# Evacuating the first layer's products by pairs of blocks, loading the first registers later, and gathering rows one part further ahead, in an attention and mixture-of-experts kernel on one core

## The chip, the core and the metric

The program runs on one core of a Trainium2 chip. The core has TensorE (PE in the rows; PEld is its weight load), VectorE (DVE), ScalarE (ACT), GpSimd (POOL) and SyncE (SP), which run side by side and wait for each other on semaphores. The metric is the device time of one execution in microseconds; a figure for a kernel is the median of its runs.

## What is computed

A random-feature attention makes 4608 rows of 512 numbers, and a mixture of eight experts is applied to these rows. Each row goes to the one expert with the largest gate value; the expert has two layers with a ReLU between them.

```python
# attention: q, k, v are 8 x 8 x 576 x 64, omega is 128 x 64
x_s = x * 64 ** -0.25                                # for x in (q, k)
h = x_s @ omega.T - sum(x_s * x_s) / 2
phi = exp(h - max(h)) / sqrt(128)
kv, z = phi(k).T @ v, sum(phi(k))
attn = (phi(q) @ kv) / (phi(q) @ z + 1e-6)
# experts: w_gate 512 x 8, w1 8 x 512 x 1024, w2 8 x 1024 x 512
logits = x @ w_gate
e = argmax(logits)
gate = softmax(logits)[e]
out[row] = gate * (relu(x[row] @ w1[e]) @ w2[e])
```

## The kernel before

The attention takes the first 250 us, and the change does not touch it. The rows of `x` go to memory (`token_rows`) as they are made. The first 256 rows of the largest expert are worked on in another form while the routing is settled (`products0` to `l21`). All other rows are sorted by expert into **parts** of 384 slots (`T3`), of which the last of an expert may be filled less. `step(t)` works on part t. On these inputs 13 parts run, t = 0 to 12.

**The split numbers.** Each operand of a product is kept as two tiles, a high part (a cast on ScalarE) and a low part (a subtraction on VectorE), and the product of two operands is the sum of high by high, high by low and low by high.

**First layer.** The 1024 hidden units are eight **blocks** f of 128. `l1` makes one block: 4 pieces of the 512 inputs by 3 products, so 12 matmuls of 128x128 weights by up to 384 rows, into one bank of PSUM. The banks are held by two tiles of two banks, `p_1[0]` and `p_1[1]`: blocks 0 and 1 share `p_1[0]`, blocks 2 and 3 `p_1[1]`, blocks 4 and 5 `p_1[0]` again, and so on. `hid` empties a block: ScalarE applies the ReLU and writes the high part to `hb` (`high_low`, L1001), then VectorE writes the low part (L1002). Dependences are followed by whole tile: whatever writes into `p_1[0]` waits for the last reader of `p_1[0]`, whichever of its two banks that read.

**Second layer.** `l2` makes 128 rows of output with 24 matmuls (8 blocks by 3 products); a full part has three of these (a = 2, 1, 0). Where a piece holds 64 rows or fewer, `l2` takes a shorter form (`half`); where a part holds 192 or fewer, the first layer does too (`slim`). Parts 8 and 12 are slim here, part 3 has 320 slots in use, the other parts run with 384.

**What stands around the layers.** The order on each engine is the order in which the code is written (the scheduling is manual).
- POOL: `gather` fetches the rows of a part from memory into `xg`, of which there are two, by three indirect transfers; `weigh` copies the gate values; `out2` scatters results by one indirect transfer for each 128 rows.
- SP: `move` writes the gathered rows to memory and reads them back in another layout (`chunk_rows`, then four transfers into `xq`). Weights of the next expert are loaded with `next(t, 1)` for the first layer and `next(t, 2)` for the second; the latter is issued when the last of the old second-layer weights has been split.
- `xrows(t + 1)`: for each of three pieces VectorE transposes (L952), ScalarE casts the high part (L57), VectorE subtracts the low part (L51). It stands in `begin`, which is written behind the second layer, or, for t = 1 and behind a part of at most 192 rows, in `layer1` behind pair g = 0.
- In a part that begins a new expert (`fresh`) the second-layer weights are split, two blocks before each pair (`split(2, ...)`, two casts and two subtractions).
- `load(t)` reads the row count of part t from `flags` into registers of the engines. `rt.plan` computes `flags` on VectorE just before part 0.

Of the kernel before, what the change touches and what calls it, by code (L numbers as in the profile page):

```python
# [18 lines left out]
P = 128  # L19
# [19 lines left out]
NCH = (NT - T2 + E * (T3 - 1)) // T3  # L39
# [377 lines left out]
class Routing:  # L417
# [99 lines left out]
    def step(self, name, product, f):  # L517

        v = {}
        def made(bank):  # L520
            v["o"] = product(bank)
        def step():
            if "o" not in v:
                made(self.bank(name))
            f(v["o"])
        step.product = made
        return step
# [263 lines left out]
class Experts:  # L791
# [193 lines left out]
            for m in (low, both) if c == NC - 1 else (both, low):  # L985
                m()

    def hid(self, f, n):
        p, k, f = self.bank1(f).unsqueeze(1), n - n % P, slice(f, f + 1)
        self.whole(f, k, p[:, :, :k])  # L990
        if k < n:
            self.half(f, p[:, :, k:n])
# [20 lines left out]
        self.half(f, y[:, :, k:k + HT])  # L1013

    def first(self, n):
        for f in range(self.NF):
            self.split(2, (f,))
            self.l1(0, f, n)
            self.hid(f, n)

    def wide(self, t, g, n):
        for f in (2 * g, 2 * g + 1):
            self.l1(t, f, n)
            self.hid(f, n)

    def slim(self, t, g):
        n = T2 - HT
# [20 lines left out]
    def layer1(self, t):  # L1048
        r = self.r1
        for g in range(self.NF // 2):  # L1050
            def fresh():
                self.split(2, (2 * g, 2 * g + 1))
                if g == self.NF // 2 - 1:
                    self.next(t, 2)
            self.when(self.new, fresh)
            wide = lambda n: lambda: self.wide(t, g, n)
            self.either(r > T2, lambda: self.either(r > T3 - HT, wide(T3), wide(T3 - HT)),
                        lambda: self.either(r > T2 - HT, wide(T2), lambda: self.slim(t, g)))
            if g == 0 and t == 1:
                self.xrows(t + 1)  # L1060
            elif g == 0:
                with self.tc.If(self.before < T2 - HT + 1):
                    self.xrows(t + 1)

# [70 lines left out]
                self.xrows(t + 1)  # L1135

    def step(self, t, following):
        if 0 < t < NCH - 2:
            self.gather(t + 2)
        if t == 0:  # L1140
            self.load(t)
            self.first(T3)
            self.l21()
            self.xrows(1)
            self.gather(2)
            self.next(0, 2)
        else:
            self.layer1(t)
        self.layer2(t)
        if t + 1 < NCH:  # L1150
            self.weigh(t + 1)
        self.nc.gpsimd.drain()
        following()
        r, r2 = self.r3, self.r2
        if t + 1 < NCH:
            self.load(t + 1)
        for a in range(A3 - 1, -1, -1):
            self.out2(t, a, r, r2)
# [108 lines left out]
```

## Time and profile before

| what | us |
| --- | --- |
| median of three runs | 810.91 |
| the three runs | 812.15, 809.96, 810.91 |
| the profiled execution, its own time | 808.02 |
| span of the profiled execution, first to last instruction | 806.3 |
| TensorE busy in the span | 684.1 (85%) |
| VectorE, ScalarE, GpSimd busy | 384.9, 367.8, 269.1 |

The rows of the trace give start, length, engine, line, operation, output and inputs; "x24" is the number of instructions merged in a row, and the bracket says how long the engine had been idle before it and which engine and line ended that. A wait on several semaphores is put down to the one that came last. TensorE's matmuls are pipelined, so the weight loads (PEld) show more exactly when work stood still.

### The profile page before, as it was taken

How to read it: one execution, taken by the hardware profiler on the slowest of the kernel's cores; microseconds unless marked ns; L12 is line 12 of the kernel's file. 1: busy time of each engine (PE TensorE's matmuls, PEld its weight loads, DVE VectorE, ACT ScalarE, POOL GpSimd, SP SyncE). 2: the span in 40 equal slices, each digit the busy share in tenths (PEclk: the TensorE clock that was granted, in tenths of full speed). 3: DMA queues.
4: the chain of work that ended last, by engine and by line, in shares of the span. 5: the costliest groups of instructions: out<-in, count | busy, mean ns of one | idle time of the engine just before them, and what ended most of it. 6: DMA issues, size and time to landing. Idle time of an engine off the chain costs nothing. (4 is left out here: it accounts for less than half of the span.)

```text
span 806.3 us, 19629 instructions
## 1 busy us (share of the span) xinstructions
PE 684.1 (85%) x7011; PEld 610.1 (76%) x7011; DVE 384.9 (48%) x777; ACT 367.8 (46%) x1130; POOL 269.1 (33%) x489
## 2 busy tenths in 40 slices
PE   8999999999999589588879695888887848579795
PEld 6999999998898378577767685777776747478684
DVE  4888888888777642331315413223422542212122
ACT  5999999999894332222223312123322422212121
POOL 6555478777776303203030301120120230020202
PEclk9999999999999899899999998999999879999998
DMA  7676357439312636403234261413352454231300
GB/s 202 183 227 222 81 178 237 136 110 338 145 39 76 180 115 209 137 9 119 43 121 135 83 176 36 133 56 85 132 189 65 127 184 134 59 111 32 94 29 22
DMA packets 92868, 100.54 MB, mean 125 GB/s; under 512 B 28702, under 2 KB 73246, under 8 KB 92064
## 3 DMA queue, kind: packets, MB, share of 16 engines
q1 hardware_dynamic: 85216, 79.27, 32.8%
q0 software_dynamic: 6800, 19.03, 7.3%
q8 instruction: 89, 1.46, 0.8%
q14 instruction: 75, 0.61, 0.3%
q10 hardware_dynamic: 688, 0.16, 0.1%
HBM read 72.12 MB, written 29.77 MB: 126 GB/s over the span
## 5 line engine op out<-in xcount | busy, mean ns | idle before, releaser
L975 PE MATMUL p<-xb,w1p 128*128 128x384 f32 (+1 forms) x1056 | 206.6, 351 | 97.2 <-DVE hb L1002 83.5
L975 PEld LDWEIGHTS p<-xb,w1p 128*128 128x128 f32 x1056 | 191.2, 199 | 112.6 <-DVE hb L1002 96.3
L1084 POOL DMA_INDIRECT out_dram<-ys,idx x38 | 38.4, 1009 | 434.1 <-DVEq L1074 263.0
L1002 DVE SCALAR_TENSOR_TENSOR hb<-p,hb 128x384 fp32r<-128x384 f32 (+1 forms) x88 | 48.0, 545 | 235.2 <-ACT hb L1001 186.7
L1001 ACT ACTIVATE hb<-p 128x384 fp32r<-128x384 f32 (+1 forms) x88 | 42.4, 482 | 193.8 <-PE p L975 191.8
L887 PE MATMUL p<-w2p,hb 128*128 128x512 f32 x552 | 127.1, 389 | 0.0
L887 PEld LDWEIGHTS p<-w2p,hb 128*128 128x128 f32 x552 | 103.6, 188 | 21.5
L191 DVE TENSOR_REDUCE mx<-pp 128x8 f32<-128x1024 f32 x64 | 78.0, 1219 | 10.4 <-PE pp L185 9.7
L199 ACT ACTIVATE qp<-pp,mx 128x128 f32<-128x128 f32 x256 | 77.3, 437 | 0.0
L199 ACT ACTIVATE kp<-pp,mx 128x128 f32<-128x128 f32 x256 | 74.2, 386 | 4.9 <-DVE de L283 1.3
L185 PE MATMUL pp<-omt,th 64*128 64x128 f32 x1024 | 71.7, 280 | 0.2 <-ACT qp_-1_320 L199 0.2
L185 PEld LDWEIGHTS pp<-omt,th 64*128 64x128 f32 x1024 | 63.0, 190 | 0.3 <-ACT qp_-1_320 L199 0.3
L887 PE MATMUL p_1tr<-w2p,hb 128*128 128x512 f32 x240 | 56.4, 390 | 0.0
L211 POOL TENSOR_TENSOR k<-kp 128x256 f32<-128x256 f32 x64 | 46.5, 727 | 24.3 <-ACT kp L199 18.9
L887 PEld LDWEIGHTS p_1tr<-w2p,hb 128*128 128x128 f32 x240 | 44.9, 188 | 9.0
L274 PE MATMUL nu<-kva,qt 128*64 128x73 f32 x1008 | 46.0, 233 | 0.0
L176 DVE COPY th<-tr 128x512 f32<-128x512 f32 x63 | 43.3, 688 | 5.6 <-PE tr L168 3.8
L57 ACT CAST xb<-xgm 128x512 fp32r<-128x512 f32 x21 | 13.0, 620 | 66.8 <-DVE xgm L952 66.8
L243 ACT COPY qt<-t 128x512 f32<-128x512 f32 x64 | 42.2, 660 | 2.0 <-PE t L168 1.6
L274 PEld LDWEIGHTS nu<-kva,qt 128*64 128x64 f32 x1008 | 36.7, 136 | 4.2
L225 PE MATMUL kf<-kp,v 128*64 128x128 f32 x512 | 39.5, 276 | 0.0
L952 DVE STREAM_TRANSPOSE xgm<-xq 128x512 f32<-128x512 f32 x21 | 22.7, 1082 | 31.1 <-DMA xq<-chunk_rows 29.6
(387 smaller groups left out, 1071.7 us busy)
## 6 DMA issues: line engine op xcount, KB each, us to landing
w1s<-in_moe_w_dram SPq DMA_DIRECT2D x5, 2048.0 KB, 8.9
w2s<-in_moe_w_dram SPq DMA_DIRECT2D x5, 2048.0 KB, 9.9
xq<-chunk_rows SPq DMA_DIRECT2D x52, 192.0 KB, 4.2
v<-in_v_dram SPq DMA_DIRECT2D x32, 256.0 KB, 5.6
token_rows<-x SPq DMA_DIRECT2D x8, 1024.0 KB, 8.2
k<-in_k_dram SPq DMA_DIRECT2D x31, 256.0 KB, 5.3
q<-in_q_dram SPq DMA_DIRECT2D x31, 256.0 KB, 5.6
chunk_rows<-xgm SPq DMA_DIRECT2D x7, 768.0 KB, 3.6
```

The source lines that it names most:

```text
L176: self.nc.vector.tensor_copy(t.rearrange("p n (a t) -> p a n t", a=2), s[("tr", h)])
L185: nc.tensor.matmul(o[:, a, n, :], t[r, n, :], self.om[r], start=True, stop=True)
L191: self.nc.vector.tensor_reduce(out=mx, in_=s[("pp", h)], axis=AX.X, op=ALU.max, negate=True)
L199: self.nc.scalar.activation(o[:, j, :], p[:, a, 2 * n + i, :], AF.Exp, bias=mx[:, a, 2 * n + i:2 * n + i + 1])
L211: nc.gpsimd.tensor_tensor(out=k2, in0=kp[:, :2, :], in1=kp[:, 2:, :], op=ALU.add)
L225: nc.tensor.matmul(pkv[c * D:(c + 1) * D, :M], vv, kk, start=n < 2, stop=n > 2)
L243: self.nc.scalar.copy(qt.rearrange("p n (a t) -> p a n t", a=2), s[("t2", h)])
L274: nc.tensor.matmul(o[r, j, :], qt[:, j, r], kva[:, h if h >= 0 else 2 * j + a, :], start=True, stop=True)
L887: self.nc.tensor.matmul(p, x, w[:, c, :], start=c == 0 and x is h and w is self.w2h, stop=c == self.NF - 1 and x is l)
L975: self.nc.tensor.matmul(o, w[:, c, k], x[:, c, :], start=i == 0, stop=i == len(ops) - 1)
L1001: self.nc.scalar.activation(h, p, AF.Relu)
L1002: self.nc.vector.scalar_tensor_tensor(out=l, in0=p, scalar=0.0, in1=h.bitcast(F32), op0=ALU.max, op1=ALU.subtract)
```

## The change

Four things are changed.
1. `hid` takes a pair of blocks. `wide` and `first` now make the products of both blocks, then one ReLU over the two banks (768 numbers for each partition in place of twice 384) and one low part. `first` splits the second-layer weights by two blocks too.
2. `load(0)` stands behind the first layer of part 0 and behind `l21`, no more ahead of them.
3. `gather(t + 2)` at the start of step t becomes `gather(t + 3)` behind `weigh(t + 1)`, ahead of the stores of part t. Step 0 now issues gathers 2 and 3.
4. `xrows` inside `layer1` stands behind pair g = 1, not g = 0.

```diff
-    def hid(self, f, n):
-        p, k, f = self.bank1(f).unsqueeze(1), n - n % P, slice(f, f + 1)
+    def hid(self, g, n):
+        p, k, f = self.p_1[g % 2], n - n % P, slice(2 * g, 2 * g + 2)
         self.whole(f, k, p[:, :, :k])
         if k < n:
             self.half(f, p[:, :, k:n])
...
     def first(self, n):
-        for f in range(self.NF):
-            self.split(2, (f,))
-            self.l1(0, f, n)
-            self.hid(f, n)
+        for g in range(self.NF // 2):
+            self.split(2, (2 * g, 2 * g + 1))
+            self.wide(0, g, n)
 
     def wide(self, t, g, n):
         for f in (2 * g, 2 * g + 1):
             self.l1(t, f, n)
-            self.hid(f, n)
+        self.hid(g, n)
...
-            if g == 0 and t == 1:
+            if g == 1 and t == 1:
                 self.xrows(t + 1)
-            elif g == 0:
+            elif g == 1:
                 with self.tc.If(self.before < T2 - HT + 1):
                     self.xrows(t + 1)
...
     def step(self, t, following):
-        if 0 < t < NCH - 2:
-            self.gather(t + 2)
         if t == 0:
-            self.load(t)
             self.first(T3)
             self.l21()
+            self.load(t)
             self.xrows(1)
             self.gather(2)
             self.next(0, 2)
...
             self.weigh(t + 1)
+        if t + 3 < NCH:
+            self.gather(t + 3)
         self.nc.gpsimd.drain()
```

**TensorE, blocks 0 and 1 of part 0.** `p_10` is `p_1[0]`, `p_11` is `p_1[1]`, `w1p0` and `w1p1` the high and low weights, `xb0` the rows of even parts. In the kernel before:

```order
L975 MATMUL p_10_6484<-xb0_6270,w1p1_6261 128x384
L975 MATMUL p_10_6484<-xb0_6270,w1p0_6260 128x384 [waits DVE_49]
L975 MATMUL p_10_6484<-xb0_6270,w1p0_6260 128x384 x3
L975 MATMUL p_10_6484<-xb0_6270,w1p0_6260 128x384 [waits DVE_49]
L975 MATMUL p_10_6484<-xb0_6270,w1p1_6261 128x384
```

In the changed kernel, first the same place, and below the dots the end of block 3 and the start of block 4:

```order
L975 MATMUL p_10_6484<-xb0_6270,w1p1_6261 128x384
L975 MATMUL p_10_6484<-xb0_6270,w1p0_6260 128x384 [waits DVE_49]
L975 MATMUL p_10_6484<-xb0_6270,w1p0_6260 128x384 x4
L975 MATMUL p_10_6484<-xb0_6270,w1p1_6261 128x384
...
L975 MATMUL p_11_6485<-xb0_6270,w1p0_6260 128x384 x4
L975 MATMUL p_10_6484<-xb0_6270,w1p0_6260 128x384 [waits DVE_49]
L975 MATMUL p_10_6484<-xb0_6270,w1p1_6261 128x384
```

The second wait on VectorE of the first fence, which stands at the first matmul of block 1, is gone from there; the next one now stands at the first matmul of block 4.

**TensorE, the last matmuls before part 0 (L877) and the register loads (L910).** In the kernel before:

```order
L877 MATMUL p_21_6259<-w2s_81,h0_6424 128x512 x3
L910 TENSOR_LOAD flags_84 [waits DVE_49]
L910 ISA x2
L910 TENSOR_LOAD flags_84
L910 ISA x2
L975 MATMUL p_10_6484<-xb0_6270,w1p0_6260 128x384 [waits DMAHW4_49,DMAHW5_49,DMAHW3_49,DMAHW6_49,DMAHW2_49,DMAHW7_49,DMAHW1_49,Activation_49]
```

In the changed kernel, the same place and, below the dots, where the loads now stand:

```order
L877 MATMUL p_21_6259<-w2s_81,h0_6424 128x512 x3
L975 MATMUL p_10_6484<-xb0_6270,w1p0_6260 128x384 [waits DMAHW4_49,DMAHW5_49,DMAHW3_49,DMAHW6_49,DMAHW2_49,DMAHW7_49,DMAHW1_49,Activation_49]
...
L887 MATMUL p_20_6258<-w2p0_6262,xb1_6271 128x512 [waits Activation_49]
L887 MATMUL p_20_6258<-w2p1_6263,xb1_6271 128x512 [waits DVE_49]
L887 MATMUL p_20_6258<-w2p0_6262,xb1_6271 128x512
L910 TENSOR_LOAD flags_84 [waits DVE_49]
L910 ISA x2
```

The register loads, with their wait for `flags`, have moved from ahead of the first layer to behind the 24 matmuls of `l21`.

**POOL, between the last store of part 0 and the gate values of part 2.** In the kernel before:

```order
L1084 DMA out_dram<-ys_6266,idx 4608x512 [waits DMASW5_49,DMASW6_49,DMASW1_49,Activation_49]
L924 DMA xgm<-token_rows,idx 128x520 [waits DMAHW0_49,DVE_49,Pool_49]
L924 DMA xgm<-token_rows,idx 128x520 [waits DVE_49,Pool_49]
L924 DMA xgm<-token_rows,idx 128x520 [waits DMASW2_49,DVE_49,Pool_49]
L930 COPY gt<-xg 128x1
```

In the changed kernel:

```order
L1083 DMA out_dram<-ys_6266,idx 4608x512 [waits DMASW1_49,DMASW2_49,DMASW0_49,Activation_49]
L930 COPY gt<-xg 128x1
L930 COPY gt<-xg 128x1 [waits DMASW3_49]
L930 COPY gt<-xg 128x1 [waits DMASW4_49]
L924 DMA xg<-token_rows,idx 128x520 [waits DMAHW7_49,DVE_49,Pool_49]
```

The three gathers stay between two groups of stores, but fetch part 4 into `xg` where part 3 was fetched into `xgm`, and stand behind the copies of the gates.

## Rows read from the trace of the kernel before

**Rows 1.** The page's heading.

```profile
span 806.3 us, 19629 instructions
```

**Rows 2.** Waits of TensorE, 268 to 806 us: who, for whom: us, times, longest.

```profile
PEld p L975 <- DVE hb L1002: 96.3, 40, 9.0
PEld p L975 <- issue: 8.1, 1, 8.1
PEld p L982 <- ACTq L1115: 7.7, 1, 7.7
PEld p L975 <- DVE hq L1002: 7.5, 4, 2.1
PE p L982 <- issue: 0.5, 1, 0.5
```

**Rows 3.** Timeline of part 2 to the start of part 3: start, length, engine, line.

```profile
368.73 2.27 PE L975 MATMUL p<-xb,w1p 128*128 128x384 f32 x12
...
371.71 0.56 DVE L1002 SCALAR_TENSOR_TENSOR hb<-p,hb 128x384 fp32r<-128x384 f32 x1 [10.03 <-ACT hb L1001]
...
372.33 4.46 PE L975 MATMUL p<-xb,w1p 128*128 128x384 f32 x24 [1.33 <-DVE hb L1002]
...
374.74 0.49 ACT L1001 ACTIVATE hb<-p 128x384 fp32r<-128x384 f32 x1 [3.13 <-PE p L975]
...
389.63 2.37 PE L975 MATMUL p<-xb,w1p 128*128 128x384 f32 x12 [1.32 <-DVE hb L1002]
...
391.85 5.64 PE L887 MATMUL p_1tr<-w2p,hb 128*128 128x512 f32 x24
...
397.33 11.04 PE L887 MATMUL p<-w2p,hb 128*128 128x512 f32 x48
...
408.21 1.92 PE L975 MATMUL p<-xb,w1p 128*128 128x320 f32 x12
```

**Rows 4.** Groups by line and shape, 360 to 807 us: busy us, mean ns.

```profile
L1002 DVE SCALAR_TENSOR_TENSOR hb<-p,hb 128x384 fp32r<-128x384 f32 x64 | 35.7, 557 | 167.4 <-ACT hb L1001 122.0 <-ACTq L1115 26.9 <-ACTq L1062 17.7
L1001 ACT ACTIVATE hb<-p 128x384 fp32r<-128x384 f32 x64 | 31.5, 492 | 144.7 <-PE p L975 143.9 <-ACTq L1115 0.7
L1002 DVE SCALAR_TENSOR_TENSOR hb<-p,hb 128x256 fp32r<-128x256 f32 x8 | 3.4, 425 | 22.7 <-ACT hb L1001 22.7
L1001 ACT ACTIVATE hb<-p 128x256 fp32r<-128x256 f32 x8 | 3.1, 384 | 12.9 <-PE p L975 11.9 <-ACTq L1115 1.0
```

**Rows 5.** Timeline before part 0: the last matmuls, the last flag, the first product.

```profile
266.12 2.74 PE L877 MATMUL p<-w2s,h 128*128 128x512 f32 x6
...
273.18 0.16 DVE L788 CAST flags<-f_sb 1x21 int32<-1x21 f32 x1
...
276.12 3.71 PE L975 MATMUL p<-xb,w1p 128*128 128x384 f32 x12 [7.27 <-issue]
```

**Rows 6.** Timeline of part 1, `xrows` inside the first layer.

```profile
328.90 1.08 DVE L952 STREAM_TRANSPOSE xg<-xq 128x512 f32<-128x512 f32 x1
...
335.68 0.49 ACT L1001 ACTIVATE hb<-p 128x384 fp32r<-128x384 f32 x1 [0.30 <-ACTq L1115]
...
337.08 6.03 PE L975 MATMUL p<-xb,w1p 128*128 128x384 f32 x24 [7.14 <-DVE hb L1002]
```

**Rows 7.** Timeline of parts 4 and 5: weights, rows of part 6, the wait.

```profile
466.61 1.30 DVE L51 TENSOR_TENSOR w2p<-w2s,w2p 128x512 fp32r<-128x512 f32 x2
...
467.93 0.41 SPq L907 DMA_DIRECT2D w2s<-in_moe_w_dram  x1
...
470.93 5.39 PEld L887 LDWEIGHTS p_1tr<-w2p,hb 128*128 128x128 f32 x24
...
479.72 1.87 SPq L945 DMA_DIRECT2D xq<-chunk_rows  x4
...
486.08 1.08 DVE L952 STREAM_TRANSPOSE xg<-xq 128x512 f32<-128x512 f32 x1 [13.70 <-DMA xq<-chunk_rows]
...
497.84 5.88 PE L975 MATMUL p<-xb,w1p 128*128 128x384 f32 x24 [8.11 <-DVE hb L1002]
```

## The prediction

> **What bounds the kernel now.** The span is 806.3 us [rows 1], the profiled execution's own time 808.02, so 1.7 us lie around the span. The change works behind 268 us, and there I read who TensorE waits for [rows 2]. The weight loads stood still for 96.3 us in 40 waits for the low part of `hb`, 7.5 us in 4 such waits of the part of 320 slots, 8.1 us ahead of part 0 and 7.7 us in a slim part. Nothing else holds them for long, so TensorE bounds this stretch, and these waits are what a change can win.
>
> Part 2 shows the plain wait [rows 3]. Block 0 runs alone (12 matmuls from 368.73), then TensorE idles 1.33 us until VectorE has ended the low part (371.71 + 0.56 = 372.27) and goes on at 372.33. Then 24 matmuls run without a gap: block 1, and block 2, which writes the other tile. Four such waits stand in a part. Twelve more matmuls in a run cost 4.46 - 2.37 = 2.09 us, 0.174 each. The first layer takes 391.85 - 368.73 = 23.1 us where 96 matmuls at that pace take 16.7. The 6.4 us between are the four waits.
>
> Three kinds of wait are longer. Ahead of part 0, the last old matmul ends at 268.86, the flags at 273.34, and the first product starts at 276.12 [rows 5]. In part 1 the three transposes and casts of `xrows` stand on ScalarE and VectorE ahead of a ReLU, and TensorE idles 7.14 us [rows 6]; part 9 has the same order. Behind a part with new weights the rows for the part after next come late: weights leave at 467.93, `xq` is asked for at 479.72, the transposes start at 486.08, and TensorE, which waits for the ReLU behind them, goes on at 497.84 after 8.11 us [rows 7]. Part 5 is shown, part 10 is alike, and the slim wait of 7.7 us is this in part 8.
>
> **The change part by part.** *Pairs.* From one 128x384 to one 128x256, ScalarE's ReLU falls by 0.108 us and VectorE's low part by 0.132 [rows 4]. On that line 768 columns take 0.492 + 3 x 0.108 = 0.82 us and 0.557 + 3 x 0.132 = 0.95. The bounds are one of the old instructions (0.49 and 0.56) and two (0.98 and 1.11); I take the line. A ReLU started 374.74 - 372.33 = 2.41 us after its block [rows 3], so with two blocks 4.5 us after the pair's start. Then 0.82, 0.1 between the engines, 0.95 and 0.06 until TensorE sees it: the tile is free 6.4 us after the pair's start. Block 4, the first to need it, is due after 48 matmuls, at 8.35. It has 1.9 us to spare, and so has every later pair. Even at the upper bounds 1.6 us are left. So the plain waits go to zero, covered by the other pair's products; without that cover, each would be dearer (rival 2). What is late next is the last pair: its low part ends 2.3 us into the second layer, which asks for it after 18 matmuls at 5.48 / 24 = 0.228 us [rows 3], at 4.1 us. So no cost there.
>
> *Registers.* The first layer of part 0 then starts where the old matmuls end, 268.9. That is the removal of the 8.1 us already counted. VectorE is busy with the flags until 273.34; then two subtractions (1.30 us, [rows 7]) and the first low part end by 275.7, and block 4 is due at 268.9 + 8.35 = 277.2, so that cover holds. At their new place the loads cost TensorE between 0 and the 2.8 us from flag to product [rows 5]. I take 0: the same loads stand between parts 2 and 3, and there the next product starts at 408.21, before the last 48 matmuls end at 408.37 [rows 3].
>
> *`xrows` behind pair 1.* In parts 1 and 9 ScalarE and VectorE have served pairs 0 and 1 before the transposes start, 10.6 us into the layer, so TensorE runs through all eight blocks. `xrows` holds ScalarE for 335.68 - 328.90 = 6.8 us [rows 6], so pair 2 is evacuated by 19.4 us and pair 3 by 20.4. The second layer starts at 16.7 and asks for them at 19.9 and 21.3: part 1 loses nothing. Part 9 also splits weights there, two pairs of casts and subtractions at 1.30 us each, and the last low part ends at 22.5; I count 1.3 us.
>
> *Gathers.* Three gathers at the same place on POOL's queue, a part earlier in purpose; step 0 gets three more. They could win at most the 13.70 us that VectorE idled ahead of the late transposes [rows 7], or lose one more such late part, 5.3 us as worked out below. I take 0: SP's `move` no longer waits for them, but where it is late it is queued behind the second-layer weights.
>
> *What stays.* The late rows. In part 4 the last weights are now split at 16.0 us into the layer: pair 2's ReLU at 12.9, 0.82 + 0.1 + 0.95, then 1.30. From there it is 479.72 - 467.93 = 11.8 to `xq`, 486.08 - 479.72 = 6.4 to the transposes and 497.84 - 486.08 = 11.8, plus 0.7 for the longer pair, to the free tile: 46.7. Part 5 starts at 16.7 + 16.4 = 33.1 and needs the tile 8.35 later, at 41.4. It waits 5.3 us. In part 9 the weights come 5.4 later (behind `xrows`), and part 10 waits 5.3 + 5.4 - 1.3 = 9.4. Before part 8, weights left 470.93 - 467.93 = 3.0 us ahead of the second layer in part 4 [rows 7], now 0.7: its slim wait grows by 2.3.
>
> *Clock.* After each long wait a run of 24 takes longer: 5.88 us [rows 7] or 6.03 [rows 6] for 4.46. Seven runs are like that; the waits in parts 5 and 10 stay, so five go, 1.5 us each: 7.5.
>
> The sum: 96.3 + 7.5 + 8.1 = 111.9, less 0.16 in each of 11 parts, since part 2's four waits of about 1.64 are 6.56 for 6.4 won (1.7), less 5.3, 9.4, 1.3 and 2.3, plus 7.5: 99 us. The profiled execution would take 808.02 - 99 = 709. It lies 2.9 below the median of 810.91, so I forecast 810.91 - 99 = **712**.
>
> A rule of the skill speaks against the change. The bubble of 1.33 us is made by a ReLU and a low part on engines that are idle most of the part [rows 3, 4]. The Trainium skill, Perfetto Trace Analysis, Optimizing Scalar/DVE Operations, says for that case that breaking instructions up may let work complete sooner; here they are merged. By that rule the time would be that of rival 2.
>
> **The rivals.** *1. Gaps at the branches.* With no waits for a semaphore, TensorE's own branches between pairs could show. Against it: block 2 follows block 1 over such a branch within the run of 24 at 0.174 [rows 3]. For it: one idle time of 0.5 us with no releaser [rows 2]. At that price for each of 40 pairs the gain shrinks by 20 to 79: 732. The Trainium skill, Runtime: NRT & Kernel Launch, Instruction fetch mechanics, states that a taken branch outside the fetched window stalls; the run of 24 shows none.
>
> *2. Slower: the merged evacuation stays on the path.* If block 2 had to wait for the low part of pair 0 (dependences following more than the tile, or the two tiles not alternating), each pair would cost the old 1.33 and 0.33 + 0.39 = 0.72 more. It decides where a pair's evacuation ends after the next pair needs its tile. 44 pairs cost 31.7 more, the register loads give 8.1: 811 + 23.6 = 835. Against it, the order of the changed kernel has no wait at block 2.
>
> *3. `xrows` still blocks.* If the release of pair 1 is only seen behind the branch that holds `xrows`, blocks 6 and 7 start at 10.6 + 7.3 = 17.9 instead of 12.5: 5.4 in parts 1 and 9, so 11 in all: 723.
>
> **How the numbers follow.** Forecast 0.80, rival 1 0.09, rival 3 0.07, rival 2 0.03, and 0.01 that gains and losses cancel. The range runs from 702, where half of the waits left goes too (21.3 with the clock of two of them), to 730, which takes in rival 3, the register loads at their upper bound, and branches at most of their price. Measurement of this kernel cannot tell less than about 0.3% from none. Faster by more is 0.96, within it 0.01, slower 0.03.
>
> **What would show it.** The first layer of parts 2, 6, 7 and 11 at 16.7 us, with runs of 96 matmuls at 0.174; one ReLU of 128x768 near 0.82 and a low part near 0.95; the first product at about 269; part 1 with no wait; waits of about 5 in part 5 and 9 in part 10. Idle time of TensorE at every pair would make rival 1 or 2 right, at block 6 of part 1 rival 3; late transposes in undisturbed parts would make my zero for the queues wrong.

## The result and the profile after

The changed kernel takes **712.41 us** (median of 4 runs, 711.83 to 714.59); the kernel before took 810.43 beside it (807.44 to 812.15). The ratio is 0.8799, with a 95% interval of 0.8767 to 0.8831. The profiled execution took 712.33 us.

The page's heading of the changed kernel, for [rows 1]:

```profile
span 710.6 us, 19585 instructions
```

Whom TensorE's weight loads wait for from 268 us on, for [rows 2] (us in all, times, longest). The 40 waits of the first layer for the low part of `hb` are gone, and so is the wait ahead of part 0; the second layer has one such wait of 0.5 us. Left in the first layer are two long waits of full parts (5 and 10) and the one of the slim part 8:

```profile
PEld p L975 <- ACTq L1061: 16.5, 2, 8.8
PEld p L982 <- ACTq L1114: 10.1, 1, 10.1
...
PEld p_1tr L887 <- DVEq L1114: 0.8, 1, 0.8
PEld p_1tr L1036 <- ACT hq L1001: 0.8, 1, 0.8
...
PEld p_1tr L887 <- DVE hb L1002: 0.5, 1, 0.5
```

The timeline of part 2, for [rows 3]. All 96 matmuls stand in one run, and the second layer follows at 357.90 - 341.23 = 16.67 us instead of 23.1. The first ReLU starts 4.52 us after the layer; its low part ends at 346.67 + 0.96 = 347.63, 6.40 after the layer's start, and the tile is due at 8.35:

```profile
341.23 16.83 PE L975 MATMUL p<-xb,w1p 128*128 128x384 f32 x96
345.75 0.81 ACT L1001 ACTIVATE hb<-p 128x768 fp32r<-128x768 f32 x1 [3.49 <-PE p L975]
346.67 0.96 DVE L1002 SCALAR_TENSOR_TENSOR hb<-p,hb 128x768 fp32r<-128x768 f32 x1 [7.28 <-ACTq L1114]
...
357.90 5.64 PE L887 MATMUL p_1tr<-w2p,hb 128*128 128x512 f32 x24
```

Both instructions among the groups by line and shape, for [rows 4] (busy us, mean ns, then idle time ahead):

```profile
L1002 DVE SCALAR_TENSOR_TENSOR hb<-p,hb 128x768 fp32r<-128x768 f32 x40 | 38.3, 957 | 127.4 <-ACTq L1114 73.1 <-ACT hb L1001 23.8 <-issue 17.1
...
L1001 ACT ACTIVATE hb<-p 128x768 fp32r<-128x768 f32 x40 | 32.5, 812 | 99.4 <-PE p L975 91.3 <-issue 3.9 <-DVE w2p L51 2.3
```

The start of part 0, for [rows 5]. The first product stands at 269.36, 5 us ahead of the last flag, and the first low part ends at 276.55, ahead of the 277.7 at which block 4 is due:

```profile
269.36 17.21 PE L975 MATMUL p<-xb,w1p 128*128 128x384 f32 x96
...
274.33 0.16 DVE L788 CAST flags<-f_sb 1x21 int32<-1x21 f32 x1
...
275.61 0.94 DVE L1002 SCALAR_TENSOR_TENSOR hb<-p,hb 128x768 fp32r<-128x768 f32 x1
```

Part 1, for [rows 6]. The transposes begin behind the second low part, 10.4 us into the layer, and the 96 matmuls of TensorE stand in one run:

```profile
308.21 16.83 PE L975 MATMUL p<-xb,w1p 128*128 128x384 f32 x96
...
317.73 0.96 DVE L1002 SCALAR_TENSOR_TENSOR hb<-p,hb 128x768 fp32r<-128x768 f32 x1 [3.20 <-ACT hb L1001]
318.61 1.10 DVE L952 STREAM_TRANSPOSE xg<-xq 128x512 f32<-128x512 f32 x1
```

Parts 4 and 5, for [rows 7], are where the wait stayed. `chunk_rows` is asked for right behind 2 MB of weights, `xq` 433.59 - 419.52 = 14.07 us after the weights, and block 4 of part 5 waits:

```profile
419.52 0.41 SPq L907 DMA_DIRECT2D w2s<-in_moe_w_dram  x1
...
420.29 0.38 SPq L943 DMA_DIRECT2D chunk_rows<-xg  x1
...
433.59 1.87 SPq L945 DMA_DIRECT2D xq<-chunk_rows  x4
...
439.80 1.08 DVE L952 STREAM_TRANSPOSE xg<-xq 128x512 f32<-128x512 f32 x1 [17.35 <-DMA xq<-chunk_rows]
...
452.53 11.36 PE L975 MATMUL p<-xb,w1p 128*128 128x384 f32 x48 [7.41 <-ACTq L1061]
```

### The profile page after: what moved, and what is told of

Same layout as the page of the kernel before. It is cut to its first block, busy times and chain, and to the rows that moved or that the text cites. A ratio compares the mean times of both kernels' runs of the same rounds, so it can differ in the third digit from the quotient of the medians.

```text
span 710.6 us, 19585 instructions
## 1 busy us (share of the span) xinstructions
PE 665.6 (94%) x7011; PEld 604.4 (85%) x7011; DVE 377.2 (53%) x729; ACT 359.2 (51%) x1082; POOL 271.3 (38%) x492
## 5 line engine op out<-in xcount | busy, mean ns | idle before, releaser
L975 PE MATMUL p<-xb,w1p 128*128 128x384 f32 (+1 forms) x1056 | 188.3, 338 | 15.9 <-ACTq L1061 15.9
L975 PEld LDWEIGHTS p<-xb,w1p 128*128 128x128 f32 x1056 | 185.9, 192 | 17.7 <-ACTq L1061 16.5
L1002 DVE SCALAR_TENSOR_TENSOR hb<-p,hb 128x768 fp32r<-128x768 f32 (+1 forms) x44 | 41.0, 933 | 145.6 <-ACTq L1114 73.1
L1001 ACT ACTIVATE hb<-p 128x768 fp32r<-128x768 f32 (+1 forms) x44 | 34.9, 793 | 108.5 <-PE p L975 100.4
```

Of the source, the lines that this page charges most:

```text
L975: self.nc.tensor.matmul(o, w[:, c, k], x[:, c, :], start=i == 0, stop=i == len(ops) - 1)
L1002: self.nc.vector.scalar_tensor_tensor(out=l, in0=p, scalar=0.0, in1=h.bitcast(F32), op0=ALU.max, op1=ALU.subtract)
```

## The experiments

Each kernel was timed beside the kernel before on the same chip, so the ratios are what compares them best. The changed kernel's ratio is 0.8799. In the diffs, dots stand for lines left out.

| kernel | us | ratio to before | 95% interval |
|---|---|---|---|
| pairs undone | 804.62 | 0.9961 | 0.9941 to 0.9981 |
| pairs alone | 734.34 | 0.9088 | 0.9058 to 0.9119 |
| registers first | 721.50 | 0.8914 | 0.8891 to 0.8936 |
| rows behind pair 0 | 711.62 | 0.8795 | 0.8776 to 0.8813 |
| gathers late | 725.58 | 0.8966 | 0.8944 to 0.8987 |
| split evacuation | 715.62 | 0.8851 | 0.8830 to 0.8873 |
| four tiles | 709.10 | 0.8776 | 0.8755 to 0.8798 |
| one ReLU more | 718.44 | 0.8864 | 0.8837 to 0.8890 |
| four ReLUs more | 769.82 | 0.9503 | 0.9476 to 0.9529 |
| rows ahead of weights | 678.85 | 0.8391 | 0.8368 to 0.8413 |
| rows ahead, four tiles | 677.52 | 0.8367 | 0.8343 to 0.8391 |
| rows ahead, gathers late | 713.51 | 0.8807 | 0.8782 to 0.8833 |

**Pairs undone.**

```
-def hid(self, g, n):
-    p, k, f = self.p_1[g % 2], n - n % P, slice(2 * g, 2 * g + 2)
+def hid(self, f, n):
+    p, k, f = self.bank1(f).unsqueeze(1), n - n % P, slice(f, f + 1)
...
 for f in (2 * g, 2 * g + 1):
     self.l1(t, f, n)
-self.hid(g, n)
+    self.hid(f, n)
```

> The changed kernel, but the ReLU and the low part stand behind each block again; registers, gathers and rows stay where the change put them. Theory (the pairs carry most of the gain): the plain waits come back, 6.4 us in each of 11 full parts, 70 us, and the rows behind pair 1 hold one block in parts 1 and 9 for some 5.5 us and a slow run behind it, 14 more; the waits in parts 5, 8 and 10 shrink since the parts are longer. 790 us (780 to 802), with some 40 waits for the low part of hb. Rival (places of rows, gathers and registers carry much of it): 760 or less.

It took 804.62: the other three edits without the pairs give 0.4% of the kernel before. The waits are those of [rows 2], but for the one ahead of part 0:

```profile
PEld p L975 <- DVE hb L1002: 98.9, 40, 9.0
PEld p L982 <- ACTq L1114: 7.8, 1, 7.8
```

The 790 was too low. I let the long waits shrink, and only the slim one did. Those in parts 1, 5, 9 and 10 are 7.5 to 9.0 us each, with matmuls at a lower granted clock behind them (0.50 at the start of each), and my sum lacked waits of 4.5, 4.1 and 3.0 us at block 1 of parts 0, 4 and 9. Nearly half of what the registers give is lost too. The first product starts 7.8 us earlier behind the old matmuls than in the kernel before (268.20), but block 1 needs the first low part, which stands behind the flags on VectorE, and the products of `l21` behind the first layer start only 4.3 us earlier:

```profile
268.20 2.65 PE L975 MATMUL p<-xb,w1p 128*128 128x384 f32 x12
...
273.17 0.16 DVE L788 CAST flags<-f_sb 1x21 int32<-1x21 f32 x1
274.45 0.54 DVE L1002 SCALAR_TENSOR_TENSOR hb<-p,hb 128x384 fp32r<-128x384 f32 x1
...
275.04 1.30 PE L975 MATMUL p<-xb,w1p 128*128 128x384 f32 x4 [4.19 <-DVE hb L1002]
```

**Pairs alone**, on the kernel before (its places of registers, rows and gathers).

> The kernel before with the pairs alone. Theory: it misses the register loads' 6.8 us (first product at 276.1 instead of 269.4) and, in parts 1 and 9, has the rows behind pair 0: the second tile is free at 15.2 us and due at 12.5, 2.7 us of waiting and 1.5 of slow run, less the 1.3 us of part 9's second layer. 712.4 + 6.8 + 4.5 = 724 us (719 to 729). Rival (the other edits matter only together with the pairs, or the late gathers cost): 735 or more.

734.34, or 74.4 less than its kernel before, and 10 more than expected. By the three single undoings below, the missing 22 us are the registers (9.1), the rows (-0.8) and the gathers (13.2), 21.5 in all. Against the expectation the gathers cost 13.2 more (I had expected nothing), the registers 2.3 more and the rows 5.3 less.

**Registers first.**

```
+self.load(t)
 self.first(T3)
 self.l21()
-self.load(t)
```

> The changed kernel with the register loads of part 0 ahead of its first layer again. Theory: the first product starts at 276.1 instead of 269.4, nothing behind it makes up for that: 719 us (717 to 721). Rival (the loads cost at either place): 712 to 714.

721.50. TensorE idles 7.27 us ahead of the first product, and the layer behind it takes longer, 18.94 us for 17.21. The granted clock is 0.50 from 279 to 283 us; the 1.7 us that this costs were not in my 719:

```profile
278.95 18.94 PE L975 MATMUL p<-xb,w1p 128*128 128x384 f32 x96 [7.27 <-issue]
```

**Rows behind pair 0.**

```
-if g == 1 and t == 1:
+if g == 0 and t == 1:
     self.xrows(t + 1)
-elif g == 1:
+elif g == 0:
```

> The changed kernel with the rows of the next part behind pair 0 again in parts 1 and 9. Theory: in each of these parts the second tile is free at 15.2 us and due at 12.5; 2.7 us of waiting at block 6 and up to 1.5 of slow run behind it, while the 1.3 us of part 9's second layer go: 717 us (715 to 721). Rival (the place does not matter, the pairs cover the rows anyhow): 712.

711.62, not told apart from the changed kernel. The expected waits at block 6 are there, 2.69 us of the weight loads in part 1 and 3.68 in part 9, with the lower clock behind them. But part 10 gives them back, so my 717 was wrong. Timeline of this kernel, end of part 9 and part 10:

```profile
592.89 6.90 PE L975 MATMUL p<-xb,w1p 128*128 128x384 f32 x24 [3.39 <-DVE hb L1002]
...
626.57 8.56 PE L975 MATMUL p<-xb,w1p 128*128 128x384 f32 x48 [2.07 <-DVEq L1061]
```

and of the changed kernel:

```profile
611.09 8.51 PE L975 MATMUL p<-xb,w1p 128*128 128x384 f32 x48
628.08 10.69 PE L975 MATMUL p<-xb,w1p 128*128 128x384 f32 x48 [8.48 <-ACTq L1061]
```

With the transposes a pair earlier, part 9's weights are asked for at 596.04 instead of 598.27, and the part ends later, so part 10's late rows cost 2.4 us instead of 8.8 and leave no lower clock behind them. In this kernel the wait was only moved.

**Gathers late.**

```
 def step(self, t, following):
+    if 0 < t < NCH - 2:
+        self.gather(t + 2)
 ...
-    if t + 3 < NCH:
-        self.gather(t + 3)
```

> The changed kernel with the gather of part t+2 at the start of step t again, ahead of the first layer instead of ahead of the stores of the step before. Theory: the transfers that read the gathered rows are asked for some 17 us later, so nothing waits: 712.4 us, within 1.5. Rival (POOL's queue is held by the stores, rows come later): 716 or more, with longer waits in parts 5, 8 and 10.

725.58, so my theory of nothing fell; the rival had the cause, but other parts. The profiled execution took 732.05, the longest of five, so its waits are on the long side. New waits stand in parts 4 (7.6 us), 7 (2.3) and 12 (5.7), where no weights precede the rows. Timeline of this kernel for part 4; part 3 starts at 373.17, part 4 at 402.93. On POOL the gathers stand behind the last store, and `chunk_rows`, `xq` and the transposes follow in a chain that ends after part 4 has begun:

```profile
387.32 0.98 POOL L1083 DMA_INDIRECT out_dram<-ys,idx  x1 [3.82 <-DVE hq L1002]
388.60 1.06 POOL L924 DMA_INDIRECT xgm<-token_rows,idx  x1 [0.30 <-issue]
...
395.00 0.39 SPq L943 DMA_DIRECT2D chunk_rows<-xgm  x1
398.69 1.84 SPq L945 DMA_DIRECT2D xq<-chunk_rows  x4
...
404.83 1.10 DVE L952 STREAM_TRANSPOSE xgm<-xq 128x512 f32<-128x512 f32 x1 [8.37 <-DMA xq<-chunk_rows]
...
418.79 10.17 PE L975 MATMUL p<-xb,w1p 128*128 128x384 f32 x48 [7.35 <-DVE hb L1002]
```

In the kernel before, the same chain had 6 us more in each part. The pairs take them away, and the earlier gathers are what keeps the chain off the path.

**Split evacuation.**

```
-p, k, f = self.p_1[g % 2], n - n % P, slice(2 * g, 2 * g + 2)
-self.whole(f, k, p[:, :, :k])
...
+k = n - n % P
+for j in range(2):
+    p, f = self.p_1[g % 2][:, j:j + 1], slice(2 * g + j, 2 * g + j + 1)
+    self.whole(f, k, p[:, :, :k])
...
```

> The changed kernel with both products of a pair first, but two ReLUs of 128x384 and two low parts behind them instead of one of each. Theory (what counts is that both products stand ahead of the tile's reading; the evacuation is covered by the other pair's products): 712.4 us, within 1.5. Rival (fewer, larger instructions save): 716 to 730, with waits for the low part. Rival (by the rule that breaking instructions up lets work complete sooner): 705 to 709.

715.62, 0.6% over the changed kernel by the ratios, whose intervals just overlap, and 3.2 us over a theory that I had put within 1.5. In no part does the first layer wait for the halves, so the theory's cause holds. But two halves take longer than the whole: in part 2 of this kernel the second ReLU starts only as the first low part ends, and the tile is free 6.74 us after the layer's start of 341.30 (347.48 + 0.56), not 6.40.

```profile
345.77 0.49 ACT L1003 ACTIVATE hb<-p 128x384 fp32r<-128x384 f32 x1 [3.44 <-PE p L975]
346.37 0.56 DVE L1004 SCALAR_TENSOR_TENSOR hb<-p,hb 128x384 fp32r<-128x384 f32 x1 [7.25 <-ACT hb L1003]
346.96 0.49 ACT L1003 ACTIVATE hb<-p 128x384 fp32r<-128x384 f32 x1 [0.70 <-DVE hb L1004]
347.48 0.56 DVE L1004 SCALAR_TENSOR_TENSOR hb<-p,hb 128x384 fp32r<-128x384 f32 x1 [0.56 <-ACTq L1116]
```

The waits that grew are the second layer's for the last halves, 4.5 us in 9 places where there were 1.3 in two. The rival that breaking up helps, at 705 to 709, is out.

**Four tiles**, evacuation behind each block as before.

```
-return self.p_1[f // 2 % 2][:, f % 2]
+return self.p_1[f % 4]
...
-    self.hid(g, n)
+        self.hid(f, n)
...
-self.p_1 = [self.pm.tile([P, 2, 512], F32, name=f"p_1{g}", tag=f"p_1{g}") for g in range(2)]
+self.p_1 = [self.pm.tile([P, 512], F32, name=f"p_1{g}", tag=f"p_1{g}") for g in range(4)]
```

> The changed kernel with the ReLU and the low part behind each block again, as in the kernel before, but with four tiles of one bank instead of two of two banks. Theory (the waits come from the dependence on a whole tile of two banks, not from the size of the evacuation): a tile is free some 3.9 us after its block's start and due after four blocks, at 8.35: no plain waits, 713 us (711 to 717). Rival (merging the ReLU and the low part is what saves): some 790 us, as with the pairs undone.

709.10, with the slim form emptied bank by bank as well: the same gain without pairs, its interval overlapping the changed kernel's. The plain waits, 6.4 us in a part, do not come back. What cost them was that block 1's products could not start before the other bank of the same tile had been read. Neither the number nor the size of the evacuating instructions did.

**One and four ReLUs more** in each pair (the diff of one; the other has 4 in its place).

```
+for _ in range(1):
+    self.nc.scalar.activation(self.hb[:, 0, f, :k], p[:, :, :k], AF.Relu)
 self.whole(f, k, p[:, :, :k])
```

> The changed kernel with the wide ReLU of each pair made twice (the same output written twice). Theory (the evacuation is covered): a pair's tile is free at 6.40 + 0.77 = 7.2 us after the pair's start and due at 8.35, and the last low part ends 3.0 us into the second layer, which asks at 4.1: 713 us (711 to 716). Rival (every lengthening of the evacuation lies on the path): 44 times 0.77, 34 us more, 746.

> The changed kernel with the wide ReLU of each pair made five times. Theory (covered up to 1.95 us, then paid): a pair's tile is free at 6.40 + 3.1 = 9.5 us, 1.1 later than due, once in a part since the pairs behind it shift with it; the last low part ends 5.3 us into the second layer, 1.2 late: 2.3 us in each of 11 full parts and some more where ScalarE also splits weights: 740 us (732 to 752). Rival (each costs in full): 44 times 3.1, 136 us more, 848.

One more takes 718.44, above the 716 that I allowed, though there is no new wait in any first layer, so the cover holds. The 6 us over the changed kernel are some 4 in the second layers, most of them in parts 1 and 9, where the transposes leave the last pair no spare time, and 3 in parts 5, 8 and 10, less 1.8 of lower clock. Four more take 769.82, 30 above expectation. In part 2 of this kernel four ReLUs take 3.34 us and the tile comes 1.31 late (expected: 1.1). The 5 ReLUs in a row take 4.2 us, no less than the pair's products (4.17), so a later pair waits a little too:

```profile
357.81 3.34 ACT L991 ACTIVATE hb<-p 128x768 fp32r<-128x768 f32 x4 [3.49 <-PE p L975]
...
363.20 4.40 PE L975 MATMUL p<-xb,w1p 128*128 128x384 f32 x24 [1.31 <-ACT hb L991]
...
367.86 4.43 PE L975 MATMUL p<-xb,w1p 128*128 128x384 f32 x24 [0.26 <-DVEq L1063]
```

My 740 counted only the latency, not ScalarE's own throughput. In a plain part that is little: parts 2, 6 and 11 are 3.0 to 3.2 us longer than in the changed kernel, where I had 2.3. Most of the 30 lies in three parts, 1 and 9 (11.3 and 11.9 longer) and 3 (8.2). In parts 1 and 9 the ten ReLUs of the last two pairs stand in a row behind the casts of `xrows`, the second layer waits 7.2 and 8.6 us for them, and its matmuls run at a granted clock of 0.50 behind that.

**Rows ahead of weights.**

```
 def begin(self, t):
-    if t + 1 < NCH:
+    if t == 1:
         self.move(t + 1)
...
             elif g == 1:
                 with self.tc.If(self.before < T2 - HT + 1):
                     self.xrows(t + 1)
+            if g == 1 and t + 2 < NCH:
+                self.move(t + 2)
```

> The changed kernel, but the rows of part t+2 are moved (chunk_rows, then xq) from inside the first layer of part t, behind the second pair, ahead of the second-layer weights on SP's queue, instead of behind the second layer's start. Theory (the waits left in parts 5, 8 and 10 come from 0.77 MB of rows queued behind 2 MB of weights): the transposes of part 6 start at about 422 us instead of 439.8, and the waits go: 7.7, 10.1 and 8.8 us, and 2.9, 1.9 and 2.2 of slow runs behind them: 712.4 - 33.6 = 679 us (675 to 688). Rival (the weights come late instead, and TensorE waits in the next part with new weights, or SP is held by xq): 695 or more, with waits behind the split of w1p or w2p.

**678.85**, 4.6% less than the changed kernel. In part 4, `xq` is asked for at 413.58, before the weights (419.14), the transposes of part 6 start at 422.70, and part 5's 96 matmuls run in one piece:

```profile
413.58 2.02 SPq L945 DMA_DIRECT2D xq<-chunk_rows  x4
419.14 0.40 SPq L907 DMA_DIRECT2D w2s<-in_moe_w_dram  x1
...
422.70 1.08 DVE L952 STREAM_TRANSPOSE xg<-xq 128x512 f32<-128x512 f32 x1 [0.63 <-DVEq L1116]
...
436.22 16.83 PE L975 MATMUL p<-xb,w1p 128*128 128x384 f32 x96
```

The waits in parts 5, 8 and 10 are gone, and no wait for late weights takes their place. This edit also asks for the rows earlier, so by itself it does not show that the place in the queue mattered. The kernel before does: behind weights `xq` follows `chunk_rows` after 11.0 to 11.2 us (three times), elsewhere after 3.6 to 4.9, as here in part 5 of the kernel before:

```profile
511.24 0.38 SPq L943 DMA_DIRECT2D chunk_rows<-xgm  x1
514.86 1.84 SPq L945 DMA_DIRECT2D xq<-chunk_rows  x4
```

So the last waits came from rows queued behind 2 MB of weights.

**Rows ahead, four tiles** (both diffs).

> Rows ahead of the weights, and four one-bank tiles with the evacuation behind each block. Theory: TensorE waits for nothing in either any more but the last low part of some parts, 1.3 us in part 9 and 0.8 in part 3, and a shorter last evacuation can win only these: 678 us (676 to 680). Rival (twice as many instructions on ScalarE and VectorE delay rows or weights): 681 to 690.

677.52, as expected, and not told apart from the last one. TensorE is busy for 97% of the span in both.

**Rows ahead, gathers late** (both diffs).

> Rows ahead of the weights, but the gathers at the start of the step again. Theory (late gathers cost because they stand on POOL behind the stores of the step before, and parts are now too short for stores, gathers, chunk_rows and xq in a row, weights or not): the waits of the kernel with late gathers in parts 4, 7 and 12 stay: 679 + 13 = 692 us (686 to 700). Rival (they cost through the queue behind the weights alone): 679 to 682.

713.51, 21 more than expected. Weights cannot be the reason for part 4's wait here, of 8.4 us, since none were asked for ahead of its rows; my rival falls. But I had only carried over three waits of the kernel with late gathers. Parts 6 (4.6 us) and 8 (7.0) wait as well, and the waits of parts 4, 6 and 8 have stretches of lower clock behind them. Even a full part is barely long enough for stores, gathers, `chunk_rows`, `xq` and transposes in a row: in part 5 (from 446.81) the first gather is at 462.99, the first transpose at 479.94, part 6 at 480.03. With the gathers late, moving the rows early gains 12 us (725.58 to 713.51); with the gathers ahead of the stores it gains 34 (712.41 to 678.85).

## Why the prediction was right

712 was forecast and 712.41 measured. The mechanism was right; that the number fits to less than a microsecond is luck, as the last point shows. The steps:

- **Plain waits to zero.** Right, with its parts: 16.67 us for the first layer, a ReLU of 0.812 and a low part of 0.957 us, a tile free at 6.40 (said: 6.4) and due at 8.35. Four tiles show that the tile was the cause, and one and four ReLUs more show the spare time from both sides.
- **Registers.** Right: the first product at 269.36 (said 268.9), no cost at the new place. Only the 8.1 was too much: that is the wait of the weight load, while the first product stood 276.12 - 268.86 = 7.26 us behind the old matmuls. Undone, the edit costs 9.1 us, 7.3 of wait and 1.7 of lower clock.
- **`xrows` behind pair 1.** Right in place (part 1 loses nothing, part 9's second layer waits 0.5 + 0.8 = 1.3), but the edit is worth nothing here: it only moves a wait between parts 9 and 10. The last low part is asked for after 20 matmuls of the second layer, where the paragraph on the pairs had 18; nothing hung on it.
- **Gathers at zero.** The number held, the reasoning lacked half. I asked what moving them wins or loses in the kernel before, and not what their old place would cost once the parts are 6.4 us shorter. That is 13 us. Had the change not moved them, my sum would have been as much too low.
- **What stays.** Part 10 waits 8.8 us (said 9.4) and part 8 10.1 (said 10.0). Part 5 waits 7.7, not 5.3: `xq` was asked for 14.07 us after the weights and not the 11.8 of [rows 7]. That term was 2.4 too small. The reason is not shown. The trace suggests the gathers, which I had put at zero: in the changed kernel those for part 7 are issued at 417.36 to 420.08, right around these weights, and in the kernel before the last gather ahead of them is issued 8.5 us earlier than they are.
- **Clock.** Mis-sized. The two stretches of lower clock left cost 11.36 - 8.51 = 2.9 and 10.69 - 8.51 = 2.2 us, where I had taken 1.5 each from runs of 24. Those runs were long enough to show it: behind part 5's wait in the kernel before the clock is back at 1.00 inside the run (last section). The stretches differ in length, and what makes one longer is not shown. Nor are the seven runs of the prediction alike; the one in part 9 of the kernel before costs 7.20 - 4.46 = 2.7:

```profile
662.23 7.20 PE L975 MATMUL p<-xb,w1p 128*128 128x384 f32 x24 [8.34 <-DVE hb L1002]
```

- **Not in the sum:** 0.8 us ahead of part 3's second layer. With 2.4 and 2.1 above, 0.8 for the registers and 0.5 at the start that is 6.6 us too slow; back come 1.2 with part 9's long slow run, 0.6 in part 10 and 0.5 in part 12, which leaves 4.3. The profiled execution, 712.33, is 3.3 above the 709 of the sum; the last microsecond lies in smaller terms. The forecast of 712 hit closer by luck: I had added the 2.9 us that the profiled execution before lay under its median, and after the change the two agree (712.33 and 712.41).

Rival 1 falls: waits with no releaser add up to some 3 us, and runs of 96 pass the branches. Rival 2 falls as a forecast, though the kernel with four ReLUs more shows the mechanism where the evacuation outgrows its cover. Rival 3 falls with part 1. The rule in the Trainium skill, Perfetto Trace Analysis, Optimizing Scalar/DVE Operations, that breaking up instructions which cause bubbles on other engines may let work complete sooner, was not borne out here. Merged, the evacuation left no plain wait; split behind the products it gave 715.62, and behind each block on separate tiles a time that cannot be told from the merged one.

Over all: the pairs alone give 74 us and the other three edits alone 4, yet together they give 98. Behind the pairs the three are worth 22 us (734.34 to 712.41), some 13 for the gathers and 9 for the registers: most of what they save became critical only once the plain waits were gone.

## What to carry to other kernels

When an engine waits for a buffer, ask first what unit the wait follows: here a tile of two banks made one bank's reader hold up the other bank's writer, and pairing the work or splitting the tile cured it alike. When a change shortens a stage, recompute every chain that had only just fitted into it (stores, gathers, transfers), and put small transfers that are needed soon ahead of large ones that are needed late on a shared queue. Edits that are worth little alone (4 us here) can keep the gain of another (22).

## What was not expected of the hardware

After a long wait the granted clock starts at its lower level. In the changed kernel, after the 7.4 us of part 5, it is 0.50 (1.2 of 2.4 GHz) for at least the first 5.5 us and 1.00 again from 460 us on. Stretches with the busy time of each engine, then the granted clock, the DMA share and GB/s:

```profile
452.50:454.00 1.50, 1.47 (x5) 1.50 (x6) 0.96 (x1) 0.01 (x1) 0.90 (x1) 0.50 0.04 11
...
456.00:458.00 2.00, 2.00 (x8) 2.00 (x7) 0.00 (x0) 0.00 (x0) 0.00 (x0) 0.50 1.00 219
...
460.00:462.00 2.00, 2.00 (x14) 2.00 (x13) 0.96 (x1) 0.72 (x1) 1.70 (x2) 1.00 0.47 127
```

In the kernel before, after the 8.11 us of part 5 [rows 7], TensorE goes on at 497.84, and the clock is 1.00 again from 501 us on, so a longer wait had the shorter stretch behind it:

```profile
500.00:501.00 1.00, 1.00 (x5) 1.00 (x4) 0.00 (x0) 0.00 (x0) 0.60 (x1) 0.50 0.00 0
501.00:502.00 1.00, 1.00 (x8) 1.00 (x6) 0.00 (x0) 0.32 (x1) 0.00 (x0) 1.00 0.68 262
```

And ReLUs in a row that write the same output take no less than one by one on ScalarE (four of 0.81 take 3.34 us), while two casts of 0.62 to different places take 1.13. Whether the output, the operation or where the input lies makes the difference is not shown.
